# One adaLN transformer block on one core: first modulation load widened, two loads on ScalarE's queue, one PSUM pool throughout

## The chip, the core and the metric

The kernel runs on one core of a Trainium2 chip. A core has TensorE (PE in the profile; its weight loads are PEld), VectorE (DVE), ScalarE (ACT), GpSimd (POOL) and SyncE (SP), which here only issues DMAs. The metric is the device time of one execution in microseconds, as the median of several runs.

## The reference

```python
mod = (_silu(c) @ w_mod).reshape(c.shape[0], 6, 1, -1)          # c (1,448), w_mod (448, 6*448)
sa, ca, ga, sb, cb, gb = (mod[:, i] for i in range(6))
h = _layernorm(x) * (1 + ca) + sa                               # x (1,2048,448), bf16
x = x + ga * A(h)     # A: q = h@wq; softmax(q k^T / 16) v per head, 16 heads of 256, 2048 cached keys; @wo
h = _layernorm(x) * (1 + cb) + sb
x = x + gb * B(h)     # B: (gelu(h@w_gate) * (h@w_up)) @ w_down, inner width 1792
return x
```

## The kernel before

Everything is bf16 with float32 accumulation. The 448 channels lie in four chunks of 128, 128, 128 and 64 partitions; the last chunk of a weight tile is padded with zeros to 128 (`wq_t`, `wm`, `wgu`). The 2048 tokens are handled in four blocks of 512 (`r`), the 2048 keys in 16 steps of 128 (`j`). Instructions run on each engine in the order in which the code emits them.

**Head start** (L145 to L325). SP issues, in this order, x of block 0, the first part of `w_mod` (`load_wm(0, 2*D)`, 896 columns), wq of head 0, k of head 0 as four transposing DMAs (two halves of the keys times two halves of the head), V of head 0, x of block 1, wo of head 0, the rest of `w_mod`, x of blocks 2 and 3, wq of head 1. `mod_cols(0)` (L176) computes the columns of `sa` and `ca` as 8 groups of 4 matmuls with one column each, `modc`; the stationary operand is always 128 columns of `wm` wide, so that the last group, which starts at column 448 + 384 = 832, reads columns 832 to 959. Then `LN` normalizes block 0: statistics on VectorE (`stats`), inverse deviation on GpSimd (`rstd`), `xn` on VectorE (`norm`), 16 PE transposes into a PSUM tile `tp`, and `hT = tp * (1+ca) + sa` on VectorE and ScalarE in turn (`transpose`). `q_proj` gives `qT`.

**Attention** (L446). A unit is one head and one block of tokens: 64 units, the blocks of a head one after another. In step `j` of a unit PE computes the scores `st` two steps ahead, ScalarE the exponential `E` one step ahead, VectorE adds `E` into `esum`, and PE accumulates `oT` (two PSUM tiles) from V and `E`. The output projection of the unit before runs in steps 0 to 7: `sums` (reciprocal of the row sums), and `wo_tile` in steps 1, 3, 5 and 7. What else is to be done hangs on a table by unit and step, `fill(u, j, f)`, whose entries run after the step's `oT` matmuls: the layer norms of blocks 1 to 3 (`add_ln`), the projections of q (also for the next head, in step 15), `mod_rep` and `scale_wo` (which multiplies wo by `ga` on GpSimd, from unit 0's step 14 on), the loads of the next head. For blocks 2 and 3 `norm` runs on GpSimd (L231).

PSUM has eight banks: `aps` gives three to `st`, two to `oT` and three to all else (`mi_tile`).

**MLP** (L478 on). After the last unit its `sums` and four `wo_tile` are emitted, the attention pools are closed, and new pools opened: `hh` (two buffers of `hhT`), `gpool`, `opl`, and the PSUM pool `mps` with four banks for gate and up tiles, two for `down` and two for the layer norm. `gate_up(r, fc)` makes one column block of the hidden layer (4 + 4 matmuls, GELU on ScalarE, product on VectorE); `down(r, t)` multiplies by `w_down`, adds x and stores. Two steps of the next block's layer norm follow each `gate_up`.

In the built program, DMA completions use eight semaphores in rotation, over all issuing engines together: a DMA is issued only when the one eight before it in program order has landed.

Of the kernel before, what the change touches and what calls it, by code (L numbers as in the profile page):

```python
# [7 lines left out]
P = 128  # L8
BF16 = mybir.dt.bfloat16
F32 = mybir.dt.float32  # L10
ACTF = mybir.ActivationFunctionType
ALU = mybir.AluOpType
# [5 lines left out]
def kernel(  # L18
# [15 lines left out]
    nc = tc.nc  # L34
    S = A_x.shape[1]
    D = A_x.shape[2]
# [6 lines left out]
    NC = S // 512  # L43
    DCH = 4
    DL = D - 3 * P
    NHC = Df // P
    inv_sqrt_dh = float(Dh) ** -0.5
    x2d = A_x[0]
    out2d = out[0]

    pool = lambda name, bufs, **kw: ctx.enter_context(tc.tile_pool(name=name, bufs=bufs, **kw))
    consts = pool("consts", 1)
    res = pool("res", 1)
    hpool = pool("hpool", 4)
    small = pool("small", 4)
    lnp = pool("lnp", 6)

    ctx.enter_context(tc.manual_schedule(engines={ET.PE, ET.Activation, ET.DVE, ET.Pool, ET.SP}))


    id_bf = consts.tile([P, P], BF16, name="id_bf")
    nc.gpsimd.memset(id_bf[:], 1.0)
    nc.gpsimd.affine_select(
# [4 lines left out]
    nc.vector.memset(ones_col[:], 1.0)  # L68
    mhalf = consts.tile([P, 4], F32, name="mhalf")
    nc.vector.memset(mhalf[:], -0.5)  # L70
    c_row = consts.tile([1, DCH * P], BF16, name="c_row")
    nc.vector.memset(c_row[:], 0.0)
    wm = res.tile([P, DCH, 6 * D], BF16, name="wm", tag="big")
    nc.vector.memset(wm[DL:P, 3, 0:2 * D + 64], 0.0)
    nc.gpsimd.memset(wm[DL:P, 3, 2 * D + 64:6 * D], 0.0)
    x_bf = [res.tile([P, 4, D], BF16, name=f"x_bf{r}") for r in range(NC)]
    x_acc = [res.tile([P, 4, D], F32, name=f"x_acc{r}") for r in range(NC)]
    ca1p_c = consts.tile([P, DCH], F32, name="ca1p_c")
    sa_c = consts.tile([P, DCH], F32, name="sa_c")
# [5 lines left out]
    att = ExitStack()  # L85
# [31 lines left out]
                )  # L117
        return kT

    def load_v(h):  # L120
        v_h = kv.tile([P, NKS, Dh], BF16, name="v_h")
        nc.sync.dma_start(out=v_h[:], in_=A_v_cache[0, h].rearrange("(s p) d -> p s d", p=P))
        return v_h

    def load_wo(h):
# [9 lines left out]

    def load_x(eng, r):
        eng.dma_start(
            out=x_bf[r][:], in_=x2d[r * 512:(r + 1) * 512, :].rearrange("(t p) d -> p t d", p=P)
        )

    def load_wm(a, b):
        nc.sync.dma_start(out=wm[:, 0:3, a:b], in_=w_mod[0:384, a:b].rearrange("(c p) n -> p c n", p=P))
        nc.sync.dma_start(out=wm[:DL, 3, a:b], in_=w_mod[384:D, a:b])
# [2 lines left out]
    warm = consts.tile([P, 1], F32, name="warm")  # L146
    nc.scalar.activation(out=warm[:], in_=ones_col[:], func=ACTF.Exp)
    load_x(nc.sync, 0)
    load_wm(0, 2 * D)
    wq, kTs, vs, wos = {}, {}, {}, {}  # L150
    wq[0] = load_wq(0)
    kTs[0] = load_k(0, parts=2)
    vs[0] = load_v(0)
    load_x(nc.sync, 1)
    wos[0] = load_wo(0)
    load_wm(2 * D, 6 * D)
    load_x(nc.sync, 2)
    load_x(nc.sync, 3)
    wq[1] = load_wq(1)
# [7 lines left out]
        )  # L167
    sg = consts.tile([P, DCH], F32, name="sg")
    nc.scalar.activation(out=sg[:], in_=cps[:], func=ACTF.Exp, scale=-1.0)
    nc.vector.tensor_single_scalar(out=sg[:], in_=sg[:], scalar=1.0, op=ALU.add)  # L170
    nc.vector.reciprocal(out=sg[:], in_=sg[:])
    scT = consts.tile([P, DCH], BF16, name="scT")
    nc.vector.tensor_tensor(out=scT[:], in0=cps[:], in1=sg[:], op=ALU.mult)
    scT_rep = consts.tile([P, DCH, P], BF16, name="scT_rep")

    def mod_cols(g0):  # L176
        mps_ = mi_tile([P, 2 * DCH], F32, "modc")
        for v in range(2):
            for m in range(DCH):
                o = (g0 + v) * D + m * P  # L180
                for k in range(DCH):
                    nc.tensor.matmul(
                        mps_[:, v * DCH + m:v * DCH + m + 1],
                        lhsT=wm[:, k, o:o + P], rhs=scT[:, k:k + 1],
                        start=(k == 0), stop=(k == DCH - 1),
                    )
        return mps_
# [123 lines left out]
        )  # L311


    modc = mod_cols(0)
    ln = LN(("a", 0), x_bf[0], ca1p_c, sa_c, mi_tile)
    for t in range(4):
        ln.stats(t)
        if t % 2 == 1:
            ln.rstd(t - 1, 2)
# [10 lines left out]
    def fill(u, j, f):  # L330
        fills.setdefault((u, j), []).append(f)
# [9 lines left out]
    fill(3, 10, lambda: mod_rep(5, gb_bf))  # L341
    fill(4, 9, lambda: mod_cols_out(mod_cols(3), sb_c, cb1p_c))

    def add_ln(u, st, key, src, c1p, s, on_pool, jn, jt):
        box = {}

        def stats(t):
            if t == 0:
                box["l"] = LN(key, src, c1p, s, mi_tile)
            box["l"].stats(t)  # L350

        def rstd():
            box["l"].rstd(0, 4)
            if on_pool:
                box["l"].shift()
        for t in range(4):
            fill(u, st[t], lambda t=t: stats(t))
        fill(u, st[3], rstd)
        for t in range(4):
            fill(u, jn[t], lambda t=t: box["l"].norm(t, on_pool))  # L360
        for p_ in range(2):
            fill(u, jt[p_], lambda p_=p_: box["l"].transpose(p_))

    for r in range(NC - 1):
        st_at = (0, 1, 2, 3) if r == 0 else (0, 2, 4, 5)
        add_ln(r, st_at, ("a", r + 1), x_bf[r + 1], ca1p_c, sa_c, r > 0,
               (5, 5, 6, 6) if r == 0 else (6, 6, 6, 6), (9, 10))
        fill(r, 12, lambda r=r: q_proj(0, r + 1))
    for u, (h, r) in enumerate(units):
        if h + 1 < H:  # L370
            if r == 0:
                def ld(h=h):
                    kTs[h + 1] = load_k(h + 1)
                    vs[h + 1] = load_v(h + 1)
                    wos[h + 1] = load_wo(h + 1)
                    if h + 2 < H:
                        wq[h + 2] = load_wq(h + 2)
                fill(u, 0, ld)
            if r == 2:
                fill(u, 0, lambda h=h: scale_wo(wos[h + 1]))  # L380
            fill(u, 15, lambda h=h, r=r: q_proj(h + 1, r))
        if h == H - 1 and r == 2:
            add_ln(u, (0, 2, 4, 6), ("b", 0), x_acc[0], cb1p_c, sb_c, False, (8, 9, 10, 11), (13, 14))


    mlpw = {}
# [88 lines left out]
                    pend = None  # L475
        pend = (h, r, oTn, sums)

    ph, pr, po, psums = pend  # L478
    pinv = psums()
    for t in range(4):  # L480
        wo_tile(ph, pr, t, po, pinv)
    att.close()


    hh = pool("hh", 2, reuse_waits="tile")
    gpool = pool("gpool", 4, reuse_waits="tile")
    opl = pool("opl", 3, reuse_waits="tile")
    mps = pool("mps", 1, space=bass.MemoryType.PSUM, reuse_waits="tile")
    wgu, wd = mlpw["gu"], mlpw["d"]

    def gate_up(r, fc, hhT):
        hr = hT[("b", r)]
        ps = []
        for i in range(2):
            p_ = mps.tile([P, 512], F32, tag="gu", bufs=4, name="gu_ps")
            o = i * Df + fc * P
            for ch in range(DCH):
                nc.tensor.matmul(  # L498
                    p_[:], lhsT=wgu[:, ch, o:o + P], rhs=hr[:, ch, :],
                    start=(ch == 0), stop=(ch == DCH - 1),  # L500
                )
            ps.append(p_)
        gl = gpool.tile([P, 512], BF16, name="gl")
        nc.scalar.activation(out=gl[:], in_=ps[0][:], func=ACTF.Gelu_apprx_tanh)  # L504
        nc.vector.tensor_tensor(out=hhT[:, fc, :], in0=gl[:], in1=ps[1][:], op=ALU.mult)  # L505

    def down(r, t, hhT):
        dps = mps.tile([P, D], F32, tag="dn", bufs=2, name="dps")
        for fc in range(NHC):
            nc.tensor.matmul(  # L510
                dps[:], lhsT=hhT[:, fc, t * P:(t + 1) * P], rhs=wd[:, fc, :],
                start=(fc == 0), stop=(fc == NHC - 1),
            )
        ob = opl.tile([P, D], BF16, name="ob")
        nc.vector.tensor_tensor(out=ob[:], in0=dps[:], in1=x_acc[r][:, t, :], op=ALU.add)  # L515
        row = r * 512 + t * P
        nc.sync.dma_start(out=out2d[row:row + P, :], in_=ob[:])

    def ln_steps(r):
        l = LN(("b", r), x_acc[r], cb1p_c, sb_c,  # L520
               lambda shape, dt, name: mps.tile(shape, dt, tag="mi", bufs=2, name=name))
        return (
            [lambda t=t: l.stats(t) for t in range(4)] + [lambda: l.rstd(0, 4)]
            + [lambda: None] + [lambda t=t: l.norm(t) for t in range(4)]
            + [lambda: None] + [lambda p_=p_: l.transpose(p_) for p_ in range(2)]
        )

    hhs = {}
    LEAD = 2
    for r in range(NC):  # L530
        if r not in hhs:
            hhs[r] = hh.tile([P, NHC, 512], BF16, name="hhT")
        todo = ln_steps(r + 1) if r + 1 < NC else []
        for fc in range(0 if r == 0 else LEAD, NHC):
            gate_up(r, fc, hhs[r])
            for _ in range(2):
                if todo:
                    todo.pop(0)()
        if r + 1 < NC:
            hhs[r + 1] = hh.tile([P, NHC, 512], BF16, name="hhT")  # L540
            for fc in range(LEAD):
                gate_up(r + 1, fc, hhs[r + 1])
        for t in range(4):
            down(r, t, hhs[r])


# [28 lines left out]
```

## Time and profile before

| what | value |
|---|---|
| median of 3 runs | 1293.74 us (1293.17 to 1294.82) |
| the profiled execution, own time | 1294.84 us |
| its span, first to last instruction | 1293.1 us |
| PE / DVE / ACT / POOL busy | 1252.4 / 773.6 / 712.9 / 84.5 us |
| mean granted TensorE clock | 0.999 |

The profile page gives busy times by engine and by group of instructions, with the idle time of the engine just ahead of a group and what ended it. The list of waits adds up who waited for whom. The timeline gives start, duration and idle time before, in order of time. The table by windows gives busy time and DMA traffic in chosen stretches. The list of DMAs gives the time from issue to landing. Durations of matmuls include their pipeline: 0.38 us each, where one starts every 0.22 us.

### The profile page before, as it was taken

What the parts mean: (1) busy time and instruction counts of PE and PEld (TensorE: products, weight loads), DVE (VectorE), ACT (ScalarE), POOL (GpSimd) and SP (SyncE); (2) the same over time, 40 slices, a digit from 0 to 9 for tenths busy, and PEclk for the clock granted to TensorE, in tenths of its full rate; (3) what the DMA queues carried; (4) which work ended last, traced back from release to release, by engine and by line L of the source; (5) the groups of instructions that cost most, each with busy time, mean ns of one, the idle gap of its engine ahead of it and who ended that gap; (6) DMA issues with size and microseconds to landing.
All of it is one profiled execution on the core that took longest, in us unless ns stands there. A gap on an engine that the chain in (4) does not pass through costs nothing. (4 is left out here: it accounts for less than half of the span.)

```text
span 1293.1 us, 17687 instructions
## 1 busy us (share of the span) xinstructions
PE 1252.4 (97%) x6132; PEld 584.3 (45%) x6252; DVE 773.6 (60%) x1601; ACT 712.9 (55%) x1228; POOL 84.5 (7%) x108
## 2 busy tenths in 40 slices
PE   2999999999999999999999999999999999999998
PEld 1444444444444444444444444444444444444444
DVE  2756556566666565766666565666665655764443
ACT  1555666666665666656566666566566666642222
POOL 1220001000102020200000000000000000000000
PEclk9999999999999999999999999999999999999999
DMA  9104030160303030303030301103030300000000
GB/s 260 38 1 80 1 72 9 34 195 7 75 1 80 1 80 1 80 1 80 1 80 2 58 23 33 48 5 76 1 80 1 73 1 1 1 1 15 15 15 15
DMA packets 95340, 52.94 MB, mean 41 GB/s; under 512 B 68113, under 2 KB 85714, under 8 KB 95250
## 3 DMA queue, kind: packets, MB, share of 16 engines
q1 hardware_dynamic: 95248, 51.80, 16.9%
q8 instruction: 49, 0.80, 0.3%
q14 instruction: 41, 0.34, 0.1%
q10 hardware_dynamic: 2, 0.00, 0.0%
HBM read 33.18 MB, written 1.84 MB: 27 GB/s over the span
## 5 line engine op out<-in xcount | busy, mean ns | idle before, releaser
L420 ACT ACTIVATE E<-st 128x512 bf16<-128x512 f32 x1024 | 597.7, 599 | 310.6 <-PE st L294 308.3
L294 PE MATMUL st<-qT,kT 128*128 128x512 bf16 x2006 | 600.3, 379 | 3.8 <-ACT qT L287 0.5
L457 DVE TENSOR_TENSOR esum<-esum,E 128x512 bf16<-128x512 bf16 x896 | 404.1, 451 | 118.5 <-ACT E L420 74.7
L460 PEld LDWEIGHTS <-v_h 128*128 128x128 bf16 x2048 | 199.8, 98 | 247.0 <-issue 3.9
L294 PEld LDWEIGHTS <-kT 128*128 128x128 bf16 x2048 | 195.3, 98 | 212.4 <-issue 1.3
L303 PE MATMUL wps<-wo_t,oTn 128*128 128x448 bf16 x512 | 138.3, 352 | 1.6 <-DVE oTn L426 0.5
L280 PE MATMUL qps<-hT,wq_t 128*128 128x512 bf16 x490 | 121.4, 382 | 1.5 <-issue 0.2
L498 PE MATMUL gu_ps<-hT,wgu 128*128 128x512 bf16 x437 | 97.8, 379 | 1.8 <-DVE x_acc_91 L308 1.2
L134 POOL TENSOR_TENSOR wo_t<-wo_t,ga_bf 128x448 bf16<-128x448 bf16 x32 | 35.5, 1130 | 880.9 <-DMA wo_t<-in_A_wo_dram 736.7
L504 ACT ACTIVATE gl<-gu_ps 128x512 bf16<-128x512 f32 x56 | 33.3, 595 | 87.7 <-PE gu_ps L498 85.5
L287 ACT CAST qT<-qps 128x512 bf16<-128x512 f32 x64 | 37.4, 585 | 76.6 <-PE qps L280 76.6
L280 PEld LDWEIGHTS <-wq_t 128*128 128x128 bf16 x512 | 50.1, 98 | 61.8 <-issue 2.3
L303 PEld LDWEIGHTS <-oTn 128*128 128x128 bf16 x512 | 50.0, 98 | 60.7 <-DVE oTn L426 0.6
L498 PEld LDWEIGHTS <-wgu 128*128 128x128 bf16 x448 | 43.5, 98 | 52.9 <-issue 1.5
L505 DVE TENSOR_TENSOR hhT<-gl,gu_ps 128x512 bf16<-128x512 bf16 x56 | 38.4, 686 | 46.2 <-PE gu_ps L498 36.1
L308 DVE SCALAR_TENSOR_TENSOR x_acc_88<-wps,inv,x_acc_88 128x448 f32<-128x448 f32 x60 | 41.1, 684 | 35.6 <-PE wps L303 35.6
L308 DVE SCALAR_TENSOR_TENSOR x_acc_90<-wps,inv,x_acc_90 128x448 f32<-128x448 f32 x60 | 41.1, 684 | 35.2 <-PE wps L303 35.2
L308 DVE SCALAR_TENSOR_TENSOR x_acc_89<-wps,inv,x_acc_89 128x448 f32<-128x448 f32 x60 | 41.1, 684 | 33.3 <-PE wps L303 33.2
L308 DVE SCALAR_TENSOR_TENSOR x_acc_91<-wps,inv,x_acc_91 128x448 f32<-128x448 f32 x60 | 40.8, 684 | 33.4 <-PE wps L303 33.4
L285 DVE CAST qT<-qps 128x512 bf16<-128x512 f32 x64 | 44.2, 691 | 26.5 <-PE qps L280 26.5
L437 DVE RECIPROCAL inv<-sps 128x4 f32<-128x4 f32 x64 | 11.7, 182 | 64.5 <-PE sps L433 64.5
L510 PE MATMUL dps<-wd,hhT 128*128 128x448 bf16 x224 | 43.0, 352 | 0.0
(330 smaller groups left out, 1087.6 us busy)
## 6 DMA issues: line engine op xcount, KB each, us to landing
wo_t<-in_A_wo_dram SPq DMA_DIRECT2D x16, 224.0 KB, 6.4
wq_t<-in_A_wq_dram SPq DMA_DIRECT2D x16, 192.0 KB, 5.2
out_dram<-ob SPq DMA_DIRECT2D x16, 112.0 KB, 1.7
wd<-in_B_w_down_dram SPq DMA_DIRECT2D x1, 1568.0 KB, 16.5
wm<-in_w_mod_dram SPq DMA_DIRECT2D x1, 1344.0 KB, 8.8
wgu<-in_B_w_gate_dram SPq DMA_DIRECT2D x1, 1344.0 KB, 8.2
wgu<-in_B_w_up_dram SPq DMA_DIRECT2D x1, 1344.0 KB, 12.3
wm<-in_w_mod_dram SPq DMA_DIRECT2D x1, 672.0 KB, 5.2
```

The source lines that it names most:

```text
L280: nc.tensor.matmul(qps[:], lhsT=wq[h][:, ch, dc * P:(dc + 1) * P], rhs=hr[:, ch, :], start=(ch == 0), stop=(ch == DCH - 1),)
L285: nc.vector.tensor_copy(out=qT[:, dc, :], in_=qps[:])
L287: nc.scalar.copy(out=qT[:, dc, :], in_=qps[:])
L294: nc.tensor.matmul(st[:], lhsT=kTs[h][:, dc, j * P:(j + 1) * P], rhs=qTs[(h, r)][:, dc, :], start=(dc == 0), stop=(dc == 1),)
L303: nc.tensor.matmul(wps[:], lhsT=oTn[:, dc, t * P:(t + 1) * P], rhs=wos[h][:, dc, :], start=(dc == 0), stop=(dc == 1),)
L308: nc.vector.scalar_tensor_tensor(out=x_acc[r][:, t, :], in0=wps[:], scalar=inv[:, t:t + 1], in1=prev[:, t, :], op0=ALU.mult, op1=ALU.add,)
L420: nc.scalar.activation(out=E[:], in_=sts.pop(g)[:], func=ACTF.Exp, scale=inv_sqrt_dh)
L457: nc.vector.tensor_tensor(out=esum[:], in0=esum[:], in1=E[:], op=ALU.add)
L460: nc.tensor.matmul(oT[i][:], lhsT=vs[h][:, j, i * P:(i + 1) * P], rhs=E[:], start=(j == 0), stop=(j == NKS - 1),)
L498: nc.tensor.matmul(p_[:], lhsT=wgu[:, ch, o:o + P], rhs=hr[:, ch, :], start=(ch == 0), stop=(ch == DCH - 1),)
L505: nc.vector.tensor_tensor(out=hhT[:, fc, :], in0=gl[:], in1=ps[1][:], op=ALU.mult)
L510: nc.tensor.matmul(dps[:], lhsT=hhT[:, fc, t * P:(t + 1) * P], rhs=wd[:, fc, :], start=(fc == 0), stop=(fc == NHC - 1),)
```

## The change

Six things are edited together.

- The first load of `w_mod` takes 2D + 64 = 960 columns instead of 896, the second the rest.
- x of block 1 and V of head 0 are issued by ScalarE instead of SP, after the exponential of `c`. `c_row` is cleared only where c is not loaded, so that its load has nothing to wait for.
- On VectorE the three small operations of silu(c) come after the statistics of the first tile of block 0, and `mod_cols(0)` is emitted after them.
- The statistics of blocks 2 and 3 move to steps 10 to 13 of the unit before (units 0 and 1), their `norm` on GpSimd to step 0 of units 1 and 2, their transposes to steps 7 and 8 (from 9 and 10), the projection to step 11 (from 12). For block 1, in unit 0, transposes move to 8 and 9 and the projection to 11.
- The MLP takes its PSUM tiles from the attention pool: gate from `st` (three banks), up from `oT` (two), `down` and layer norm from the three of `mi_tile`. The pools stay open to the end. The last unit's `sums` and `wo_tile` become steps between the first `gate_up` calls.
- x is one tile, `x_all`, which shares two buffers with `hhT`; `gpool` has three buffers instead of four, `opl` two instead of three.

```diff
+    c_row = consts.tile([1, DCH * P], BF16, name="c_row")
+    nc.vector.memset(c_row[:, D:], 0.0)
...
-    c_row = consts.tile([1, DCH * P], BF16, name="c_row")
-    nc.vector.memset(c_row[:], 0.0)
...
+    WA = 2 * D + 64
...
-    x_bf = [res.tile([P, 4, D], BF16, name=f"x_bf{r}") for r in range(NC)]
+    x_all = res.tile([P, NC * 4, D], BF16, name="x_all", tag="xh", bufs=2)
+    x_bf = [x_all[:, 4 * r:4 * r + 4, :] for r in range(NC)]
...
-    load_wm(0, 2 * D)
+    load_wm(0, WA)
...
     kTs[0] = load_k(0, parts=2)
-    vs[0] = load_v(0)
-    load_x(nc.sync, 1)
     wos[0] = load_wo(0)
-    load_wm(2 * D, 6 * D)
+    load_wm(WA, 6 * D)
...
     nc.scalar.activation(out=sg[:], in_=cps[:], func=ACTF.Exp, scale=-1.0)
+    load_x(nc.scalar, 1)
+    vs[0] = load_v(0, nc.scalar)
...
-    modc = mod_cols(0)
     ln = LN(("a", 0), x_bf[0], ca1p_c, sa_c, mi_tile)
     for t in range(4):
+        if t == 1:
+            silu_c()
+            modc = mod_cols(0)
         ln.stats(t)
...
-        st_at = (0, 1, 2, 3) if r == 0 else (0, 2, 4, 5)
-        add_ln(r, st_at, ("a", r + 1), x_bf[r + 1], ca1p_c, sa_c, r > 0,
-               (5, 5, 6, 6) if r == 0 else (6, 6, 6, 6), (9, 10))
-        fill(r, 12, lambda r=r: q_proj(0, r + 1))
+        if r == 0:
+            add_ln(0, 0, (0, 1, 2, 3), ("a", 1), x_bf[1], ca1p_c, sa_c, False, (5, 5, 6, 6), (8, 9))
+        else:
+            add_ln(r, r - 1, (10, 11, 12, 13), ("a", r + 1), x_bf[r + 1], ca1p_c, sa_c, True,
+                   (0, 0, 0, 0), (7, 8))
+        fill(r, 11, lambda r=r: q_proj(0, r + 1))
...
-    ph, pr, po, psums = pend
-    pinv = psums()
-    for t in range(4):
-        wo_tile(ph, pr, t, po, pinv)
-    att.close()
-
-    hh = pool("hh", 2, reuse_waits="tile")
-    gpool = pool("gpool", 4, reuse_waits="tile")
-    opl = pool("opl", 3, reuse_waits="tile")
-    mps = pool("mps", 1, space=bass.MemoryType.PSUM, reuse_waits="tile")
...
-            p_ = mps.tile([P, 512], F32, tag="gu", bufs=4, name="gu_ps")
+            p_ = aps.tile([P, 512], F32, tag=("st", "oT")[i], bufs=(3, 2)[i], name="gu_ps")
...
-        dps = mps.tile([P, D], F32, tag="dn", bufs=2, name="dps")
+        dps = mi_tile([P, D], F32, "dps")
...
-            hhs[r] = hh.tile([P, NHC, 512], BF16, name="hhT")
+            hhs[r] = res.tile([P, NHC, 512], BF16, name="hhT", tag="xh", bufs=2)
         todo = ln_steps(r + 1) if r + 1 < NC else []
+        if r == 0:
+            ph, pr, po, psums = pend
+            box = {}
+            todo = (
+                [lambda: None, lambda: box.update(inv=psums())]
+                + [lambda t=t: wo_tile(ph, pr, t, po, box["inv"]) for t in range(4)] + todo
+            )
```

More of the change, by code (lines that the diff above doesn't have):

```diff
@@ L55 @@
     small = pool("small", 4)
+    gpool = pool("gpool", 3)
+    opl = pool("opl", 2)
     lnp = pool("lnp", 6)
     ctx.enter_context(tc.manual_schedule(engines={ET.PE, ET.Activation, ET.DVE, ET.Pool, ET.SP}))
+    c_row = consts.tile([1, DCH * P], BF16, name="c_row")
+    nc.vector.memset(c_row[:, D:], 0.0)
     id_bf = consts.tile([P, P], BF16, name="id_bf")
@@ L70 @@
     nc.vector.memset(mhalf[:], -0.5)
-    c_row = consts.tile([1, DCH * P], BF16, name="c_row")
-    nc.vector.memset(c_row[:], 0.0)
     wm = res.tile([P, DCH, 6 * D], BF16, name="wm", tag="big")
-    nc.vector.memset(wm[DL:P, 3, 0:2 * D + 64], 0.0)
-    nc.gpsimd.memset(wm[DL:P, 3, 2 * D + 64:6 * D], 0.0)
-    x_bf = [res.tile([P, 4, D], BF16, name=f"x_bf{r}") for r in range(NC)]
+    WA = 2 * D + 64
+    nc.vector.memset(wm[DL:P, 3, 0:WA], 0.0)
+    nc.gpsimd.memset(wm[DL:P, 3, WA:6 * D], 0.0)
+    x_all = res.tile([P, NC * 4, D], BF16, name="x_all", tag="xh", bufs=2)
+    x_bf = [x_all[:, 4 * r:4 * r + 4, :] for r in range(NC)]
     x_acc = [res.tile([P, 4, D], F32, name=f"x_acc{r}") for r in range(NC)]
@@ L118, in load_k, with load_v @@
         return kT
-    def load_v(h):
+    def load_v(h, eng=nc.sync):
         v_h = kv.tile([P, NKS, Dh], BF16, name="v_h")
-        nc.sync.dma_start(out=v_h[:], in_=A_v_cache[0, h].rearrange("(s p) d -> p s d", p=P))
+        eng.dma_start(out=v_h[:], in_=A_v_cache[0, h].rearrange("(s p) d -> p s d", p=P))
         return v_h
@@ L137, in load_x @@
         eng.dma_start(
-            out=x_bf[r][:], in_=x2d[r * 512:(r + 1) * 512, :].rearrange("(t p) d -> p t d", p=P)
+            out=x_bf[r], in_=x2d[r * 512:(r + 1) * 512, :].rearrange("(t p) d -> p t d", p=P)
         )
@@ L169, with silu_c @@
     nc.scalar.activation(out=sg[:], in_=cps[:], func=ACTF.Exp, scale=-1.0)
-    nc.vector.tensor_single_scalar(out=sg[:], in_=sg[:], scalar=1.0, op=ALU.add)
-    nc.vector.reciprocal(out=sg[:], in_=sg[:])
+    load_x(nc.scalar, 1)
+    vs[0] = load_v(0, nc.scalar)
     scT = consts.tile([P, DCH], BF16, name="scT")
-    nc.vector.tensor_tensor(out=scT[:], in0=cps[:], in1=sg[:], op=ALU.mult)
+    def silu_c():
+        nc.vector.tensor_single_scalar(out=sg[:], in_=sg[:], scalar=1.0, op=ALU.add)
+        nc.vector.reciprocal(out=sg[:], in_=sg[:])
+        nc.vector.tensor_tensor(out=scT[:], in0=cps[:], in1=sg[:], op=ALU.mult)
     scT_rep = consts.tile([P, DCH, P], BF16, name="scT_rep")
@@ L342, with add_ln @@
     fill(4, 9, lambda: mod_cols_out(mod_cols(3), sb_c, cb1p_c))
-    def add_ln(u, st, key, src, c1p, s, on_pool, jn, jt):
+    def add_ln(u, us, st, key, src, c1p, s, on_pool, jn, jt):
         box = {}
@@ L356, in add_ln @@
         for t in range(4):
-            fill(u, st[t], lambda t=t: stats(t))
-        fill(u, st[3], rstd)
+            fill(us, st[t], lambda t=t: stats(t))
+        fill(us, st[3], rstd)
         for t in range(4):
@@ L382 @@
         if h == H - 1 and r == 2:
-            add_ln(u, (0, 2, 4, 6), ("b", 0), x_acc[0], cb1p_c, sb_c, False, (8, 9, 10, 11), (13, 14))
+            add_ln(u, u, (0, 2, 4, 6), ("b", 0), x_acc[0], cb1p_c, sb_c, False, (8, 9, 10, 11), (13, 14))
     mlpw = {}
@@ L519, in ln_steps @@
     def ln_steps(r):
-        l = LN(("b", r), x_acc[r], cb1p_c, sb_c,
-               lambda shape, dt, name: mps.tile(shape, dt, tag="mi", bufs=2, name=name))
+        l = LN(("b", r), x_acc[r], cb1p_c, sb_c, mi_tile)
         return (
@@ L539 @@
         if r + 1 < NC:
-            hhs[r + 1] = hh.tile([P, NHC, 512], BF16, name="hhT")
+            hhs[r + 1] = res.tile([P, NHC, 512], BF16, name="hhT", tag="xh", bufs=2)
             for fc in range(LEAD):
@@ L544 @@
             down(r, t, hhs[r])
+    att.close()
 _INS = ['A_x', 'A_k_cache', 'A_v_cache', 'A_wq', 'A_wo', 'B_x', 'B_w_gate', 'B_w_up', 'B_w_down', 'c', 'w_mod']
```

## The prediction

> **What bounds the kernel now.** I began with busy times and the 40 slices of the page.
>
> ```profile
> PE 1252.4 (97%) x6132; PEld 584.3 (45%) x6252; DVE 773.6 (60%) x1601; ACT 712.9 (55%) x1228; POOL 84.5 (7%) x108
> PE   2999999999999999999999999999999999999998
> DMA  9104030160303030303030301103030300000000
> ```
>
> PE is busy everywhere but in the first slice (32 us) and the change removes no matmul, so only PE's idle time can be won: 1293.1 - 1252.4 = 40.7 us. The list of PE's waits says where it is named:
>
> ```profile
> PE modc L182 <- DMA wm<-in_w_mod_dram: 18.1, 4, 14.9
> PE cps L164 <- DMA c_row<-in_c_dram: 4.4, 1, 4.4
> PE tp L252 <- POOL xn L231: 3.1, 6, 0.6
> PE gu_ps L498 <- DVE x_acc_91 L308: 1.2, 1, 1.2
> ```
>
> The timeline of the head start (start, duration, engine, instruction; in brackets idle time and its end) shows the largest at work:
>
> ```profile
> 1.30 0.49 SPq L142 DMA_DIRECT2D wm<-in_w_mod_dram  x1
> ...
> 7.29 0.83 PE L182 MATMUL modc<-scT,wm 128*128 128x1 bf16 x25 [0.48 <-DMA wm<-in_w_mod_dram]
> ...
> 14.17 0.47 SPq L142 DMA_DIRECT2D wm<-in_w_mod_dram  x1
> ...
> 23.04 0.24 PE L182 MATMUL modc<-scT,wm 128*128 128x1 bf16 x3 [14.93 <-DMA wm<-in_w_mod_dram]
> 24.03 0.19 PE L182 MATMUL modc<-scT,wm 128*128 128x1 bf16 x1 [0.75 <-DMA wm<-in_w_mod_dram]
> 24.26 0.16 DVE L190 COPY sa_c<-modc 128x4 f32<-128x4 f32 x1 [15.78 <-PE modc L182]
> ...
> 30.97 0.38 PE L294 MATMUL st<-qT,kT 128*128 128x512 bf16 x1
> ...
> 32.89 0.38 PE L460 MATMUL oT_265<-E,v_h 128*128 128x512 bf16 x1
> ```
>
> 28 of 32 `modc` matmuls are done at 8.1 us; the last four read columns 896 to 959, which belong to the second load, issued at 14.17 and landed at 23 and 24. From `sa_c` (24.26) a chain of 8.6 us with no long wait leads to the first `oT` (32.89).
>
> For the units I read the first start of their `oT` tiles (first and last start stand after the durations):
>
> ```profile
> L460 PE MATMUL oT_495<-E,v_h x16: 376/379/634, 52.7 to 74.6; 128*128 128x512 bf16 x16
> L460 PE MATMUL oT_728<-E,v_h x16: 376/379/379, 77.2 to 97.5; 128*128 128x512 bf16 x16
> L460 PE MATMUL oT_963<-E,v_h x16: 378/379/379, 100.1 to 115.4; 128*128 128x512 bf16 x16
> ```
>
> Unit 0 starts at 32.9, so units 0, 1, 2 take 19.8, 24.4 and 22.9 us; unit 5 (136.0 to 153.1) takes 17.1.
>
> **What the Trainium skill says.** "DMA: Bandwidth & Descriptors", section "Issuing engines are not separate DMA queues": DMAs of all engines run on the same 16 DMA engines, a second issuer saves only issue time; section "Queues, rings and completion order": each DMA engine takes turns between the queues it has work for, packet by packet. So ScalarE's two loads bring no bandwidth, but overtake what waits on SP's queue. No run so far shows it: in the trace before, ScalarE issues only c. "TensorE: Matmul & The Clock Gate", section "What's actually happening": an idle window of some 3.4 us halves the clock. The trace agrees in kind: the `qps` matmuls after the idle stretch take 609 ns in the mean, 382 over the whole run.
>
> **Part A, the head start.** The wider load takes the second load out of `modc`'s way. In the changed program the last four weight loads of `modc` have no wait left. What comes next has two legs.
> - w_mod: its second DMA landed at 1.85 + 5.4 = 7.25. It grows with the first from 784 to 840 KB: 56 KB at the 280 GB/s of 2 to 4 us is 0.2 us. x of block 1 is now issued by ScalarE at about 4.9 (its exponential ends at 4.85) and takes turns with it; 0.88 MB have moved by then (280 and 371 GB/s), so 0.44 MB of x0 and w_mod are left, and an equal share for x1 costs at most 0.44 / 0.37 = 1.2 us. I take 0.8. It lands at 8.2; 29 matmuls at 0.83 / 25 are 1.0; `sa_c` at 9.4.
> - LN: GpSimd's last `rs` ended at 8.87 + 0.72 = 9.6. The statistics may start when x0 lands (0.80 + 3.7 = 4.5) instead of 5.46, but silu's three operations (0.7 with gaps) now lie after the first: 9.3.
>
> So `sa_c` moves from 24.26 to 9.4: 14.8 us. The chain behind it is unchanged if its loads are there: first score at 16.2, first `oT` at 18.1. k: the first two transposes landed at 8.6 and 10.0; they now wait for c and x0 (about 4 and 4.5 us), and sharing with ScalarE's loads at most doubles what is left of their way: 14. The fourth waits for x1 to land (about 10) and then needs 4 to 5 us; its half is used six steps after 18.1. V: landed at 17.0, issued at 10.64; now issued at about 5.6. Upper bound: all that was queued up to wo (4.2 MB with k, V, x1, wo) had landed at 12.97 + 6.1 = 19.1, plus 0.2; lower bound: 16.3, without the last transpose and wo (0.49 MB at the 198 GB/s of 8 to 12 us: 2.5) and the gaps in issue (0.5: DMA share 0.76 from 12 to 14 us). I take 17.5, just in time. The rest of w_mod is now held on SP's queue until V has landed, with x2, x3 and wq1 behind it; with its 9.3 us it lands at 27, and `mod_rep` needs it at 48.07 - 14.8 = 33.3. x2 would land at 24.8 (empty queue) to 28.4 (9.6 as before); VectorE wants it at 27.9, and its `esum` additions have eight `E` buffers of cover. ScalarE's issue (0.5 to 1.4 us each) ends before it is needed at 12.2. Cost nothing. A: **-14.8**, from -11.5 (V at 19.3, PE losing its clock) to -15.3.
>
> **Part B, units 1 and 2.** Beyond a plain unit they hold a projection (8 x 0.216 = 1.7) and 16 transposes (two gaps of 0.66 in unit 0's timeline: 1.3), so 20.1 us explain themselves, and 4.3 and 2.8 do not. GpSimd finishes `xn` (four of 0.77) only while PE already transposes: 1.5 us of waits each, and in unit 1 a slow clock after it (`oT` up to 634 ns, window clock 0.93). Unit 0, where VectorE norms, has only 19.8 - (17.1 - 1.6 without wo and sums + 1.7 + 1.3 + 0.9 for `mod_rep`) = 0.4 left over. With the statistics a unit ahead `xn` is ready some 3 us before step 7. Gain 4.3 + 2.8 - 2 x 0.4 = 6.3. On the other side: four bn_stats pairs (0.80 each) enter VectorE's queue in unit 0, ahead of the `ga` copy, and GpSimd's `rs` and shift (some 2 us) now stand before `scale_wo` (2.26): done about 54.5 in the old clock, where the first `wo_tile` starts at 54.1: 0.4 (0 to 1.0). B: **-5.9**, from -4 to -6.6.
>
> **Part C, attention to MLP.** From the last `oT` (1143.27, next free slot 1143.49) to the first `gu_ps` (1147.32) pass 3.8 us with 1.6 us of work (4 sums, 8 `wps` at 0.19): idle 2.2. Now the gate tile finds an `st` bank free, the up tile an `oT` bank whose copy ended at 1144.16, during the gate's 0.86 us; wo goes in between. The GELU table load (1.28, ends 1145.56) puts the first product at 1146.9; the third up tile needs its bank at about 1148. C: **-2.2**, from -1.2 to -2.4.
>
> **Nothing**: c's earlier load (w_mod is later than c anyway); three `gl` and two `ob` buffers (a column takes 1.73 us against 0.6 + 0.7 of use, a `down` tile 2.65 against a store of 1.7); `hhT` in x's buffer (x is last read about unit 4, the second `hhT` is written after 1143). If a cover fails it shows as waits of PE in `gate_up`.
>
> **Sum.** -14.8 - 5.9 - 2.2 = -22.9, against the profiled execution's 1294.84: 1271.9. The median lies 1.1 lower: 1270.8, rounded to **1271.0**.
>
> **Rivals.**
> - DMA takes over: V or k arrives late because x1 and V share with w_mod and k; PE waits at its first `st` or `oT` for some 3 us and starts slowly. For: the DMA share is 0.9 to 1.17 from 4 to 24 us, and the margin for V is 0.6 us. Against: the bytes due by then landed at 19.1 even with gaps in their issue. A falls to -11.5, and with a clock lost for longer B to -5: about 1276.
> - The change doesn't do what it says: `modc` waits on the later load after all. Then B and C alone: about 1286. The missing wait in the program speaks against.
> - Slower, by PSUM in the MLP: two `oT` banks for up tiles let an up tile wait for the product two columns back. Now the product ends 1.7 us before (up ends, product 0.69 + 0.2; the next but one up begins 2.6 after). From a product 1.7 us late each of 56 columns waits; 2.1 us late eats the 22.9 (0.41 x 56), 2.2 us gives about 1298. Against: the four `gu` banks had the same depth, two columns.
>
> **How the numbers follow.** The forecast 0.75, DMA 0.17, not done 0.02, a loss that just eats the gain 0.02, slower 0.04. The bounds of the parts give 1269 to 1277, DMA reaches higher: 1268 to 1280. A measurement of this kernel tells 0.2% (2.6 us) from no change; faster by more than that 0.94, within 0.02, slower 0.04.
>
> **What would show it.** After: `sa_c` near 9.4, the first `oT` near 18, no PE wait on w_mod after 9 us; units 1 and 2 near 20.5 us without waits of `tp` on POOL; the first `gu_ps` right behind the last `oT`. A PE wait on v_h or kT of over 1 us speaks for DMA; waits of `gu_ps` on `hhT` for the PSUM rival; either makes the prediction wrong.

## The result, and the profile after

| | before | after |
|---|---|---|
| median | 1293.70 us (4 runs, 1293.17 to 1294.82) | 1271.94 us (4 runs, 1271.70 to 1272.13) |
| profiled execution, own time / span | 1294.84 / 1293.1 us | 1272.12 / 1270.4 us |
| first `oT` | 32.89 us | 16.86 us |
| units 0, 1, 2 | 19.82, 24.45, 22.95 us | 19.87, 21.39, 20.71 us |

The ratio is 0.9831 (95% interval [0.9814, 0.9848]), 21.8 us less, against 1271.0 (1268 to 1280) predicted. The page of the changed kernel, its busy times and slices:

```profile
PE 1248.1 (98%) x6133; PEld 583.1 (46%) x6252; DVE 774.7 (61%) x1601; ACT 712.9 (56%) x1229; POOL 85.2 (7%) x108
PE   7999999999999999999999999999999999999998
DMA  9103030713030210303030403021020300000000
```

PE's work is the same, its first slice went from 2 tenths to 7. PE idles for 1270.4 - 1248.1 = 22.3 us instead of 40.7. The list of PE's waits of the changed kernel (us in total, times, longest):

```profile
PE modc L189 <- DMA wm<-in_w_mod_dram: 4.8, 2, 4.7
PE cps L166 <- DMA c_row<-in_c_dram: 2.1, 1, 2.1
PE tp L259 <- DVE xn L244: 1.1, 2, 0.6
...
PE wps L310 <- POOL wo_t L138: 0.5, 1, 0.5
```

The wait of 14.9 us on w_mod is gone, and so are the waits of `tp` on GpSimd. A wait on w_mod of 4.7 us ahead of the first `modc` stays. New is a wait on the scaled wo. The timeline of the changed head start:

```profile
2.44 0.48 ACTq L141 DMA_DIRECT2D x_all<-in_A_x_dram  x1
2.77 0.16 ACT L171 ACTIVATE sg<-cps 128x4 f32<-128x4 f32 x1
3.14 0.85 ACTq L126 DMA_DIRECT2D v_h<-in_A_v_cache_dram  x1
...
7.46 0.93 PE L189 MATMUL modc<-scT,wm 128*128 128x1 bf16 x29 [0.15 <-DMA wm<-in_w_mod_dram]
8.43 0.16 DVE L197 COPY sa_c<-modc 128x4 f32<-128x4 f32 x1 [0.29 <-PE modc L189]
8.54 0.77 POOL L228 TENSOR_TENSOR rs<-rs,mhalf 128x2 f32<-128x2 f32 x1
...
15.03 0.38 PE L301 MATMUL st<-qT,kT 128*128 128x512 bf16 x1
15.25 0.10 PEld L301 LDWEIGHTS <-kT 128*128 128x128 bf16 x1 [0.42 <-DMA kT<-in_A_k_cache_dram]
16.86 0.38 PE L471 MATMUL oT_268<-E,v_h 128*128 128x512 bf16 x1
```

The last 29 of the 32 `modc` matmuls now run in one go at 7.46, and `sa_c` comes at 8.43 instead of 24.26. The first `oT` follows 8.43 us later (8.63 before). A k transpose is the last load that anything in this chain waits for: 0.42 us, on a weight load that runs ahead of PE.

The rows of the `oT` tiles of units 1, 2 and 3 (duration min/median/max in ns, then first and last start):

```profile
L471 PE MATMUL oT_517<-E,v_h x16: 376/379/379, 36.7 to 55.5; 128*128 128x512 bf16 x16
L471 PE MATMUL oT_750<-E,v_h x16: 376/379/379, 58.1 to 76.2; 128*128 128x512 bf16 x16
L471 PE MATMUL oT_966<-E,v_h x16: 378/379/379, 78.8 to 94.2; 128*128 128x512 bf16 x16
```

From one row's first start to the next's, units 1 and 2 take 21.4 and 20.7 us, and no matmul takes 634 ns any more. The timeline where attention ends:

```profile
1122.02 0.38 PE L471 MATMUL oT_11357<-E,v_h 128*128 128x512 bf16 x1
1122.24 1.89 PE L499 MATMUL gu_ps<-hT,wgu 128*128 128x512 bf16 x8
```

The first gate matmul stands directly behind the last `oT`, where 4.05 us lay between their starts before.

In this one pair of profiled executions the span can be cut at landmarks: up to the first `oT` it lost 32.89 - 16.86 = 16.0 us, in units 1 and 2 5.3, from the last `oT` to the last `ob` (the last vector operation, ahead of the last store) 146.67 - 144.45 = 2.2, together 23.5. From the start of the last `ob` to the end of the span it took 3.9 us instead of 3.2. That leaves 22.7, the difference of the spans.

### The profile page after: what moved, and what is told of

It is laid out like the page before. It is cut to its first block, busy times and chain, and to the rows that moved or that the text cites. A ratio compares the mean times of both kernels' runs of the same rounds, so it can differ in the third digit from the quotient of the medians.

```text
span 1270.4 us, 17681 instructions
## 1 busy us (share of the span) xinstructions
PE 1248.1 (98%) x6133; PEld 583.1 (46%) x6252; DVE 774.7 (61%) x1601; ACT 712.9 (56%) x1229; POOL 85.2 (7%) x108
## 4 chain that ended last, share of the span: by engine, by line
PE 96%; DVE 2%; issue 1%; ACT 1%; POOL 0%; DMA 0%; DVEq 0%; POOLq 0%
PE st L301 34%; PE qps L287 9%; PE wps L310 8%; PE gu_ps L499 8%; PE dps L511 3%; DVE esum L468 1%; PE tp L259 1%; PE sps L444 0%; ACT E L431 0%; DVE bst L220 0%; DMA x_all<-in_A_x_dram 0%; PE oT_10996 L471 0%; PE oT_5507 L471 0%; PE oT_4121 L471 0%; PE oT_4814 L471 0%
```

## The experiments

**Theory**: the three parts act on PE's path one after another and add; w_mod is nearly all of A, and ScalarE's queue only keeps what comes next in time. **Rivals**: the gain of A needs the second queue (the wide load alone leaves a later wait); B comes from something other than the place of the norm; the parts overlap. The first four kernels are the kernel before with one part of the change each.

**The wide load alone.**

```diff
-    load_wm(0, 2 * D)
+    load_wm(0, 2 * D + 64)
-    load_wm(2 * D, 6 * D)
+    load_wm(2 * D + 64, 6 * D)
```

> The kernel before with only the first load of w_mod widened to 960 columns; x of block 1 and V stay on SP's queue. Theory (the wait on the second load was the whole of the head start's gain): sa_c at about 8.5, the first oT at about 17.2, with V just landed at 17.0 as before; 15.7 us less, median about 1278. Rival (ScalarE's queue is needed, otherwise V is the next wait): PE waits for v_h over 1 us, first oT later than 18.5, median 1280 or more.

Measured: 1279.45 us (ratio 0.9885 [0.9871, 0.99]), 14.5 less than the 1293.97 of the kernel before beside it. `sa_c` came at 8.54, the first `oT` at 17.51. Two numbers in the code make two thirds of the whole gain, and need no second queue. One later wait does show: VectorE stood 3.3 us for x of block 1 (landed at 18.25), and unit 0 took 20.47 us instead of 19.82.

**ScalarE's queue alone.**

```diff
-    vs[0] = load_v(0)
-    load_x(nc.sync, 1)
 ...
     nc.scalar.activation(out=sg[:], in_=cps[:], func=ACTF.Exp, scale=-1.0)
+    load_x(nc.scalar, 1)
+    vs[0] = load_v(0, nc.scalar)
```

> The kernel before with only x of block 1 and V of head 0 on ScalarE's queue; the first load of w_mod stays at 896 columns. Theory: the last modc matmuls still wait for the second load, which is now held until V has landed (about 14) and lands at about 23; sa_c at 23 to 24.5, median 1292.5 to 1294.5. Rival (the early start of V and x is itself worth something): first oT earlier by 3 us or more, median below 1291.

Measured: 1296.64 us (1.0021 [1.0012, 1.003]): 2.7 us more. The timeline of its profile has `sa_c` here:

```profile
25.39 0.16 DVE L190 COPY sa_c<-modc 128x4 f32<-128x4 f32 x1 [16.67 <-PE modc L182]
```

That is 1.1 us later than before: the second w_mod load, which everything waits for, lands later. Only 0.25 of it reached the first `oT` (33.14), because the `qps` matmuls behind it ran 0.8 us quicker than in the profile of the kernel before, and units 1 and 2 had no stretch at a lower clock (shown below), which is worth another 1.5. Other kernels show that both vary from one execution to the next, and this one (1293.91) was the quickest of its 11 runs. So the 1.1 us can well be part of the 2.7; where the rest lies is open. The loss itself holds at equal mean clock: the two runs at 1.0 took 1293.91 and 1295.04, the two such runs of the kernel before 1291.38 and 1292.13. Without the wide load the second queue gains nothing.

**The place of the norm alone**: `add_ln` and its calls as in the change, nothing else.

```diff
-            fill(u, st[t], lambda t=t: stats(t))
-        fill(u, st[3], rstd)
+            fill(us, st[t], lambda t=t: stats(t))
+        fill(us, st[3], rstd)
 ...
+            add_ln(r, r - 1, (10, 11, 12, 13), ("a", r + 1), x_bf[r + 1], ca1p_c, sa_c, True,
+                   (0, 0, 0, 0), (7, 8))
```

> The kernel before with only the new places of the layer norms of blocks 1 to 3 in units 0 to 2. Theory: units 1 and 2 take 21.4 and 20.7 us as in the changed kernel, with a wait of about 0.5 on POOL's scale_wo in unit 1; 5.2 us less, median about 1288.5. Rival (the units were slow because of the clock after the long head start, not because of GpSimd's norms): less than 2.5 us, median above 1291.

Measured: 1288.06 us (0.9953 [0.9938, 0.9968]), 5.9 less. Units 1 and 2 took 21.38 and 20.73 us, the changed kernel's to 0.02 us. Its list of PE's waits has the new wait of the changed kernel, and none of `tp` on GpSimd:

```profile
PE wps L303 <- POOL wo_t L134: 0.5, 1, 0.5
```

The 5.9 us are not all of units 1 and 2, which give 5.3 in this profile. Although the MLP's code is the old one here, its first gate matmul starts 2.87 us after the last `oT` (1137.94) instead of 4.05, without the wait of 1.2 us on `x_acc_91` that the kernel before has:

```profile
1140.81 5.99 PE L500 MATMUL gu_ps<-hT,wgu 128*128 128x512 bf16 x26
```

Why that wait goes with the norm's place isn't shown.

**The MLP in the attention pool alone**: banks, pools, `x_all`, the last unit's work between the gate tiles.

```diff
-            p_ = mps.tile([P, 512], F32, tag="gu", bufs=4, name="gu_ps")
+            p_ = aps.tile([P, 512], F32, tag=("st", "oT")[i], bufs=(3, 2)[i], name="gu_ps")
 ...
-        dps = mps.tile([P, D], F32, tag="dn", bufs=2, name="dps")
+        dps = mi_tile([P, D], F32, "dps")
```

> The kernel before with only the MLP part: PSUM tiles from the attention pool, the last unit's sums and wo between the first gate_up, x as one tile, hhT in its buffers, gl and ob with three and two buffers. Theory: the first gu_ps follows the last oT without a gap, 2.2 us less, median about 1291.5. Rival (what the change lost at the end, 0.8 us after the last store's issue, comes from the two ob buffers or the shared PSUM): only 1.4 less, about 1292.3, with 3.3 us instead of 2.5 from the last ob to the end.

Measured: 1292.0 us (20 runs; 0.9985 [0.9978, 0.9991]), 2.0 less, with no gap ahead of the first `gu_ps`. The three gains are 14.5, 5.9 and 2.0: 22.4 us against 21.8 for the whole change. So they add within the noise, since each ratio's interval is 1 to 2 us wide to either side. The traces show that one piece is counted twice: the 1.2 us at the start of the MLP come with the norm's place alone and with the MLP alone, and the whole change has them once. The queue's part is what can't be seen in that sum.

These four, with the kernel before, show a term of B that doesn't repeat. The table by windows for units 1 and 2, of the kernel before (first two lines), of ScalarE's queue alone (next two) and of the MLP alone (columns: length, then busy us and instructions of PE, PEld, DVE, ACT and POOL, PE's clock, DMA share, GB/s):

```profile
52.70:77.20 24.50, 22.37 (x108) 10.42 (x109) 15.01 (x34) 11.94 (x22) 7.51 (x11) 0.93 0.00 1
77.20:100.10 22.90, 20.84 (x107) 9.61 (x108) 14.16 (x33) 11.85 (x22) 5.60 (x10) 1.00 0.00 1
```

```profile
52.96:75.90 22.94, 20.88 (x108) 9.64 (x108) 15.48 (x34) 11.89 (x22) 7.50 (x11) 1.00 0.00 1
75.90:98.84 22.94, 20.88 (x107) 9.65 (x108) 14.20 (x33) 11.88 (x22) 5.60 (x10) 1.00 0.00 1
```

```profile
52.70:76.54 23.84, 22.18 (x108) 10.23 (x108) 15.20 (x34) 11.89 (x22) 7.51 (x11) 0.93 0.00 1
76.54:100.38 23.84, 22.17 (x108) 10.19 (x108) 14.19 (x33) 11.89 (x22) 5.61 (x10) 0.93 0.00 1
```

Attention is the same in these three. At full clock a unit takes 22.94 us; a stretch at a lower clock (mean 0.93 over the unit) adds 0.9 to 1.5 us and fell into unit 1, into neither, or into both. The wide load alone had it in unit 2 (24.20 us, clock 0.93). The mean clocks over whole runs fit this: below 1.0 in 44 of the 46 runs of the kernel before beside these experiments, and 1.0 in all four runs with the place of the norm alone. So such a stretch is the usual case, not the exception.

The other kernels are the changed one with one edit.

**The narrow load put back.**

```diff
-    load_wm(0, WA)
+    load_wm(0, 2 * D)
-    load_wm(WA, 6 * D)
+    load_wm(2 * D, 6 * D)
```

> The changed kernel with the first load of w_mod narrowed back to 896 columns. Theory: the last modc matmuls wait again, for a load held on SP's queue until V has landed (about 14), issued at about 16 and landed at 23.5 to 25; sa_c 15.5 to 17 later than in the changed kernel, units and MLP as there, median about 1288 (1287 to 1290). Rival (part of the gain is due to the early DMAs on ScalarE's queue): below 1285.

Measured: 1287.74 us (0.9951 [0.9936, 0.9966]), 15.8 above the changed kernel, with `sa_c` at 24.25. Its list of PE's waits has the old wait again:

```profile
PE modc L189 <- DMA wm<-in_w_mod_dram: 20.4, 4, 14.9
```

**V and x of block 1 back on SP's queue.**

```diff
+    vs[0] = load_v(0)
+    load_x(nc.sync, 1)
     wos[0] = load_wo(0)
 ...
-    load_x(nc.scalar, 1)
-    vs[0] = load_v(0, nc.scalar)
```

> The changed kernel with x of block 1 and V of head 0 back on SP's queue, in the old order. Theory (ScalarE's queue is worth nothing, V lands just in time from SP): first oT at 16.9 to 17.6, median within 0.8 us of the changed kernel, 1271.5 to 1272.8. Rival (the second queue hides V): PE waits for v_h, median 1274 or more.

Measured: 1273.37 us (0.9838 [0.9824, 0.9853]), 1.4 above the changed kernel; the intervals of the two ratios overlap, so the trace has to tell. V was issued at 10.75 and landed at 16.8, before the first `oT` at 17.49 (later than in the changed kernel by slower `qps` matmuls, not by a load). The late one was x of block 1, in VectorE's timeline:

```profile
18.64 0.63 DVE L220 BATCH_NORM_STATS2 bst<-x_all 128x6 f32<-128x448 bf16 x1 [3.81 <-DMA x_all<-in_A_x_dram]
```

VectorE stood for 3.81 us with `esum` queued behind this, and unit 0 took 21.29 instead of 19.87: 1.42 us.

**V alone back on SP's queue**, x of block 1 left on ScalarE's; beside it the changed kernel once more (1272.5 us, first `oT` 16.53).

```diff
+    vs[0] = load_v(0)
     wos[0] = load_wo(0)
 ...
-    vs[0] = load_v(0, nc.scalar)
```

> The changed kernel with V of head 0 on SP's queue behind k, and only x of block 1 on ScalarE's. Theory (of the two loads it is x of block 1 that the queue helps, since VectorE waited 3.8 for it in e6_changed_sp_queue): unit 0 at 19.9, V landed at about 17, first oT at 16.9 to 17.6, median within 0.8 of the changed kernel. Rival (V is what had to be early): PE waits for v_h, first oT 17.8 or later, median 1 us or more above the changed kernel.

> The changed kernel again, unaltered, on the chip of the other runs of this set, for comparison: about 1272.0, first oT at 16.6 to 17.5 by the state of TensorE's clock, units 1 and 2 at 21.4 and 20.7.

Measured: 1273.24 us, 0.7 above the changed kernel beside it; the intervals of the ratios, 0.984 [0.9827, 0.9853] and 0.9834 [0.9821, 0.9848], overlap. The traces do tell them apart. The timeline with V on SP:

```profile
12.16 0.81 SPq L126 DMA_DIRECT2D v_h<-in_A_v_cache_dram  x1
...
18.50 0.60 PE L471 MATMUL oT<-E,v_h 128*128 128x512 bf16 x2 [0.88 <-DMA v_h<-in_A_v_cache_dram]
```

Here V is what PE waits for. It was issued 1.4 us later than with both loads on SP. In both, V stands behind the fourth k transpose, and SP took 8.08 us to issue the four transposes here, 6.69 there. The difference is in the second one (3.91 us instead of 2.65): the third went out at 9.05, before x of block 1 landed at 9.5 (2.39 + 7.1), and the fourth right behind it. So the rotation of eight semaphores isn't what held V; why the issue took longer is open. Unit 0 took 19.87 again. Left on SP, x of block 1 costs a wait of VectorE (1.4 us of unit 0 above, 0.65 with the wide load alone), and V, issued late, a wait of PE of 0.9. With both on SP, V was in time; x of block 1 alone on SP wasn't tried.

**One more load on ScalarE's queue**: x of block 2 between x of block 1 and V.

```diff
-    load_x(nc.sync, 2)
 ...
     load_x(nc.scalar, 1)
+    load_x(nc.scalar, 2)
```

> The changed kernel with x of block 2 also on ScalarE's queue, between x of block 1 and V: 448 KB more that take turns with k. Theory (the head start now ends at the transposed k, whose second transfer landed at 15.25 against its use at 15.8): k lands 1.2 to 2 us later, PE waits for kT, first oT at 18 to 18.8, median about 1273.3. Rival (the DMAs have slack, LN and PE's clock bound the head start): first oT unchanged within 0.4, median 1271.5 to 1272.4.

Measured: 1274.67 us (0.9851 [0.9835, 0.9868]; 1272.09 to 1275.57). In the head start of its profile a wait of PE on k appears:

```profile
16.43 1.25 PE L301 MATMUL st<-qT,kT 128*128 128x512 bf16 x5 [0.50 <-DMA kT<-in_A_k_cache_dram]
```

and the first score matmul, at 15.54, had stood 0.62 us before that, which the profile puts down to a VectorE instruction ending then; its weight load waited 1.11 for k. The first `oT` came at 17.52. The units after it were as in the changed kernel, and the profiled execution was the quickest of four, so the other 2.3 to 3.5 us of the slower runs stay open. The direction holds in the trace: 448 KB more on the second queue, and k is late.

**`scale_wo` ahead of the inverse deviation on GpSimd** (unit 0, step 14), to take away the new wait.

```diff
-        fill(us, st[3], rstd)
+        fill(us, 14 if us != u else st[3], rstd)
```

> The changed kernel with GpSimd's inverse deviation and shift for blocks 2 and 3 one step later (step 14), so that in unit 0 scale_wo of head 0 comes first. Theory: the wait of wps on scale_wo (0.5, and 0.65 between the starts of its two matmuls) goes, xn still is ready before step 7; unit 1 takes 20.7 instead of 21.4, median about 1271.3. Rival (the later xn is now late for the transposes of step 7, or VectorE is what holds unit 1): a wait of tp on POOL, no gain or a loss.

Measured: 1271.38 us (0.9823 [0.9809, 0.9838]). The wait of `wps` on `wo_t` is gone and unit 1 takes 20.72 us, as unit 2: 0.67 less. The median is 0.6 lower, which these runs don't separate from the changed kernel (the changed kernel itself had 1271.94 and 1272.5).

**The same, with silu and `modc` ahead of the first statistics.**

```diff
-        if t == 1:
+        if t == 0:
             silu_c()
             modc = mod_cols(0)
```

> e7_scale_first with silu(c) ahead of the statistics of block 0 again: its exponential ends at 2.93, and VectorE idles until x0 lands at 4.5. Theory (behind modc, LN's inverse deviation at 9.3 is the head start's later leg, and the transposed k close behind at 15.25): rs ends at 8.7, the wait of tp on xn shrinks from 0.46 to nothing, first oT 0.3 to 0.6 earlier, at about 16.2, unless k is late; unit 1 at 20.7; median about 1271.0. Rival (k bounds already): first oT unchanged at 16.6 to 16.9, PE waits for kT, median 1271.4.

Measured: 1272.0 us (0.983 [0.9817, 0.9844]). In its timeline the layer norm's last `rs` starts 0.58 us earlier, and `sa_c` doesn't move:

```profile
7.96 0.72 POOL L228 TENSOR_TENSOR rs<-rs,mhalf 128x2 f32<-128x2 f32 x1
8.48 0.16 DVE L197 COPY sa_c<-modc 128x4 f32<-128x4 f32 x1 [0.91 <-PE modc L189]
```

The `qps` matmuls start at 12.08, in the changed kernel at 12.09. That doesn't mean that the layer norm's leg has slack. GpSimd clears part of `hT` right behind `rs`, and an `xn` of VectorE that runs beside this clearing takes longer. Here it is the first `xn`:

```profile
8.62 0.77 DVE L244 TENSOR_SCALAR xn<-x_all,mv,rs 128x448 bf16<-128x448 bf16 x1
8.74 0.52 POOL L253 MEMSET hT<- 64x512 bf16 x1
```

In the changed kernel it is the third, which started when `rs` was ready (9.31), beside the clearing at 9.37:

```profile
9.34 0.68 DVE L244 TENSOR_SCALAR xn<-x_all,mv,rs 128x448 bf16<-128x448 bf16 x1
```

The four of the kernel before, with no clearing beside them, took 0.39 us each. So the earlier `rs` moved the slow `xn` from the third place to the first, and the transposes ended at the same time. A kernel with the clearing elsewhere wasn't tried. No version was shown to be faster than the changed kernel.

## Why the prediction was right, step by step

The sum was -22.9 against the profiled execution; the spans differ by 22.7. The medians differ by 21.8: the profiled execution lay 1.1 above its median before, and only 0.2 after. Some of the agreement is errors that cancel, which is luck.

- **A, -14.8 predicted, -16.0 in the traces** (-14.5 for the wide load alone, 15.8 lost without it). The step w_mod was mis-sized. The widening was put at 0.2 us and sharing with x of block 1 at 0.8; the second DMA landed at 1.85 + 5.6 = 7.45, 0.2 later than before, so sharing cost nothing that can be seen (the widened second DMA took 5.4 and 5.7 us from issue to landing with both loads on SP's queue, and 5.4 to 5.6 with one or more on ScalarE's). `sa_c` at 8.43 instead of 9.4 is 1.0 of the 1.2 us.
- **The chain behind `sa_c`, "unchanged": right by luck.** From `sa_c` to the first `oT` it took 8.43 us instead of 8.63, but two terms cancel. Up to the first `qps` it grew from 3.15 to 3.66 us: the LN leg was sized right (its last `rs` ended at 9.31, forecast 9.3), but the third `xn` had to wait for it and then ran slowly beside GpSimd's clearing. From the first `qps` to the first score it shrank from 3.56 to 2.94, which varies between executions of the changed kernels.
- **"x of block 1 is now issued by ScalarE at about 4.9" failed.** It went out at 2.44, V at 3.14. The forecast took the old time of the exponential, which waited for c; c's own load, put under "Nothing", lands at 2.13 instead of 4.40 because it no longer waits for the clearing of its row: it was issued at 0.80 instead of 1.27. PE's wait for it also ended sooner after its issue (1.3 us against 3.1), and why isn't shown. So that edit was not nothing: V landed at 13.9, not 17.5, and VectorE had x of block 1 by 9.7. The margin for V, which the forecast called "just in time", is 3 us.
- **k, "at most doubles what is left: 14": too early.** SP needed 11.8 us to issue the four transposes instead of 6.6, and the second landed 9.7 us after its issue instead of 5.0; the first half of k was complete only at 15.2. The fourth went out at 14.2, long after x of block 1 had landed (9.7), so the wait that the forecast counted for it didn't bind; SP's slow issue did. The matmul that reads it started at 15.78, when ScalarE had its `qT` ready, so the margin was about half a us. The rival "DMA takes over" was close, through k and not through V; one load more on that queue makes it a wait of 0.5 us of PE.
- **B, -5.9 predicted, -5.3 in the traces, -5.9 for the norm's place alone.** Of this last, 1.2 lie at the start of the MLP in its trace. The mechanism is as described. The residue per unit is 0.6 instead of 0.4 (20.7 against 20.1), and `scale_wo` costs 0.67 instead of 0.4. And 1.5 of the old 24.45 us was the stretch at a lower clock, which the sum booked as steady: at full clock the gain is 2 x 22.94 - 21.39 - 20.71 = 3.8. The rest is the slow stretch, whose length depends on the run.
- **C, -2.2 predicted and measured**: from the last `oT` to the last `ob` it is 2.2 less. Half of it, 1.2, goes with the norm's new place too, as that experiment showed, which the forecast didn't see. PE has no wait of any `gu_ps` in the MLP, so the rival with two `oT` banks did not come.
- **Nothing**: the smaller `gl` and `ob` buffers and `hhT` in x's buffer show no wait. The slower tail (3.9 us) isn't theirs: the MLP alone, with the same two `ob` buffers, has 3.2; over all profiles it lies between 3.1 and 3.9.
- **ScalarE's queue**, of which the prediction said that it brings no bandwidth but overtakes: by the table by windows the core moved from 2 to 20 us 2 x 0.280 + 4 x (0.294 + 0.198 + 0.261 + 0.365) = 5.0 MB before and 2 x 0.272 + 4 x (0.320 + 0.256 + 0.266 + 0.261) = 5.0 MB after. That agrees with what the prediction cites from the Trainium skill, "DMA: Bandwidth & Descriptors", section "Issuing engines are not separate DMA queues": the order of landing changed, not the amount. Those that were overtaken paid: k as above, and the two loads of wq took 7.4 us from issue to landing instead of 5.3 and 4.9; they landed at 10.5, 1.6 us before `qps`.

## What to carry to other kernels

When an engine waits long for a load, look which bytes of it the waiting instruction reads: here 64 columns in a load one place further back held PE for 15 us, and two constants freed it. After such a wait is gone, size the next legs by the queue's new times, not the old ones: here an earlier small load (c) moved everything issued behind it. The second queue gave no more bytes here; decide what it shall overtake, and look at what is overtaken, by leaving out one load at a time. When an experiment moves one instruction, see what else on its engine moves along: the earlier `rs` took the clearing behind it with it, and the gain was gone. And when single edits are added up, look in each trace where its gain lies, since two of them can win the same microsecond.

## What was not expected of the hardware

- ScalarE's queue issued x of block 1 at 2.44, 0.33 us before the exponential that stands ahead of it in the code starts (2.77).
- With V and x of block 1 on another queue, the second k transpose took 9.3 to 9.9 us to land in the profiles of the changed kernel and its versions, instead of 4.7 to 5.1 with both on SP's queue, and the wq loads, issued at the same time as x of block 1, took 7.4 us instead of 5.3 and 4.9; the w_mod loads, issued ahead of it, lost little or nothing (5.6 and 5.7 us against 5.4 and 5.2).
- An `xn` of VectorE took 0.67 to 0.77 us where GpSimd's clearing of `hT` (0.52) ran beside it, and 0.38 or 0.39 with nothing beside it, in the head start and in unit 0 of the profiles of both kernels and in the one with silu first. What the two engines share isn't shown.
- The eight `qps` matmuls after the idle head start took 2.8 to 3.0 us in some profiles and 3.7 to 3.9 in others, with nothing ahead of them in the traces that goes with it: from `sa_c` to the first `oT` it was 8.43 and 8.26 in two executions of the changed kernel, 9.24 in the one with silu first. What decides it is open.
- The lower clock in units 1 and 2 came in four of eight such units (unit 1 before, unit 2 with the wide load, both with the MLP alone; neither with ScalarE's queue alone), all in kernels where PE's transposes wait for GpSimd's `xn`, several stops of under 1 us within a few us, and in no profile with the norm moved. The Trainium skill, "TensorE: Matmul & The Clock Gate", section "A second HAM failure mode: psum-queue depth-cycling", tells of a kernel whose clock goes down and up because PE stops briefly between groups of matmuls. The low clock with short stops agrees with that in kind; the stops here are on `xn`, and that they cause it wasn't tried by themselves.
